# Attending and feeding forward the last 512 queries as two halves of 256, in a transformer block on one Trainium2 core

## Chip, cores, metric

One core of one Trainium2 chip runs the whole program. The metric is device time in microseconds of one launch; medians of several runs are quoted. The first profile of the kernel before was taken at a granted TensorE clock of 0.749 and spans 1417.9 us, where the timed runs take 1201 us.

In the profiles PE is TensorE (PEld its weight loads), ACT is ScalarE, DVE is VectorE and POOL is GpSimd. PSUM is the memory that this kernel's matmuls write, in eight banks.

## The reference

A pre-layernorm transformer block: 2048 tokens, width 1024, 32 heads of 32, feed-forward width 3584, bfloat16.

```python
x = A_x                                         # 1 x 2048 x 1024
h = x + attention(layernorm(x)) @ wo            # qkv = layernorm(x) @ wqkv, 32 heads, full softmax
out = h + gelu(layernorm(h) @ w1 + b1) @ w2 + b2
```

## The kernel before

The program builds a graph of tasks (groups of instructions with what they read and write), plans it with a list scheduler that has a price for each task, and emits each engine's instructions in the order of that plan. The plan's times do not reach the chip; only the order does.

Queries go in four chunks of 512 (`qc`). For each chunk and pair of heads, PE computes scores in row tiles (contraction of 32), ACT takes exponentials of 128 x 1024 at a time (256 of them per chunk), and PE multiplies these with V and with ones, in column tiles ("PV"). The output projection (`wo`), layernorm and feed-forward of chunk `qc - 1` are background: they fill PE's time inside the attention of chunk `qc`. There they have one PSUM bank (bank 7; banks 0 to 5 hold scores, 6 the sums of PV), and use four weight tiles of 32 columns side by side, so that they share a tiling mode with PV. The last chunk has no attention after it; its `wo`, layernorm and feed-forward are the tail, with eight banks and the full 128 x 128 array.

```python
# (cut) a background matmul: narrow while attention runs, full in the tail
if narrow:   # four 32-column tiles, side by side: "a group"
    for j in range(4): p.matmul(psum[32*j:32*j+32, bank, c0:c1], lhsT[:, 32*j:32*j+32], rhs, tile_position=(0, 32*j), ...)
    pe(fns, occ, ..., mode="col")
else:
    pe(lambda p: p.matmul(psum[:, bank, c0:c1], lhsT, rhs, ...), occ, ..., mode="full")

# (cut) the order of the program
for qc in range(1, NCH):
    ...
    wo(R1, qc - 1, [7], R1); ln2(R1, qc - 1, [7], ...); ffn1(R1, qc - 1, [7]); ffn2(R1, qc - 1, [7])
    attention_chunk(qc)
    attention_flush()
al = [0, 1, 2, 3, 4, 5, 6, 7]
wo(R1, NCH - 1, al, R2); ln2(R2, NCH - 1, al); ffn1(R2, NCH - 1, al); ffn2(R2, NCH - 1, al)

# (cut) who gets PE next, in the plan
if "qk" in best: return best["qk"]                                   # scores first
...
if "pv" in best and (... waiting >= PV_FORCE ...): return best["pv"]
if "bg" in best: return best["bg"]                                   # what is left: background
```

In the plan a change of PE's tiling mode (row tiles, column tiles, full array) costs 0.1 us (`switch=0.1`) and a group of 512 columns 0.2195 us.

The softmax here doesn't subtract the row's maximum and nothing guards it: scores larger than these inputs give would overflow.

Of the kernel before, what the change touches and what calls it, by code (L numbers as in the profile page):

```python
# [284 lines left out]
def build_kernel(nc, A_x, A_wqkv, A_wo, B_w1, B_b1, B_w2, B_b2, out):  # L285
# [72 lines left out]
    PT, B_PT = sb(top, "PT", [P, NPT, 2, 512], BF, NPT)  # L358
    ot_lo = Area(top.cur)
# [19 lines left out]
    gT, B_gT = sb(ffn, "gT", [P, FC, 512], BF, FC)  # L379

    class Rings:


        def __init__(self, area, pfx, nw1, nw2, ngl, nos, nx, nxb):
# [3 lines left out]
            self.w1, self.B_w1 = sb(area, pfx + "w1r", [P, nw1, DC, 256], BF, nw1)  # L388
            w2_area = Area(area.cur + 3 * 4096)
            self.w2, self.B_w2 = sb(area, pfx + "w2r", [P, nw2, 4, 512], BF, nw2)  # L390

            if nw2 == 7:
                self.xq, self.B_xq = sb(w2_area, pfx + "xq", [P, DC, 512], BF)
                self.hnT, self.B_hnT = sb(w2_area, pfx + "hnT", [P, DC, 512], BF, 1, 4)
            self.xb, self.B_xb = sb(area, pfx + "xb3", [P, self.nxb, D], BF, self.nxb)
# [171 lines left out]
    def load_q(qc, g):  # L567
        n = qc * G + g
        s = n % NQ
        if n < 2:  # L570
            return
        for half in range(2):
            dma(QT2[64 * half:64 * half + 64, s, :, :], qd[g, qc].rearrange("(pr r) t -> r pr t", pr=2), 64 * 2048,
                reads=[B_qd[g][qc]], writes=[B_QTh[s][half][0], B_QTh[s][half][1]], prio=-1)

    def late_q(R, qc, gs):

        dma(R.xq[:, :, :], xd[qc - 1], P * 8192, reads=[B_xd[qc - 1]], writes=[R.B_xq], prio=0)
        for g2 in range(gs // 2, G // 2):
            s = wblock(R, A_wqkv[:, 256 * g2:256 * g2 + 256], 0)  # L580
            for k in range(2):
                g = 2 * g2 + k
                for dc in range(DC):
                    mm(7, R.w1[:, s, dc, k * P:k * P + P], R.xq[:, dc, :], dc == 0, dc == DC - 1,
                       [R.B_w1[s], R.B_xq], True)
                o = R.next("os", R.nos)
                dve(lambda v, o=o: v.tensor_copy(R.ost[:, o, :], psum[:, 7, :]), c_dve_ps(512),
                    reads=[B_ps[7]], writes=[R.B_ost[o]])
                dma(qd[g, qc], R.ost[:, o, :], P * 1024, reads=[R.B_ost[o]], writes=[B_qd[g][qc]], prio=0)
# [19 lines left out]
    class Att:  # L609


        def __init__(self):
# [4 lines left out]
            self.fin = set()  # L617

        def qk(self, qc, units):

            fns, banks, rd, us = [], [], [], []
            for p16, kt in units:
                tc, k4 = divmod(kt, 4)
                half, i = divmod(k4, 2)
                g, pr = divmod(p16, 2)
                qs = (qc * G + g) % NQ
                u = self.unit % self.n_units
                self.unit += 1
                us.append(u)
                for j in range(2):  # L630
                    r0 = 64 * half + 32 * j

                    def fn(p, j=j, r0=r0, u=u, p16=p16, tc=tc, i=i, qs=qs, pr=pr):
                        return p.matmul(psum[:, 2 * u + j, :], KT2[r0:r0 + 32, p16, tc, i, :],  # L634
                                        QT2[r0:r0 + 32, qs, pr, :], start=True, stop=True, tile_position=(r0, 0))
                    fns.append(fn)
                banks += [B_ps[2 * u], B_ps[2 * u + 1]]
                rd += [B_KT[4 * p16 + tc][half], B_QTh[qs][half][pr]]
            pe(fns, 0.224, reads=rd, writes=banks, kind="qk", mode="row")
            for (p16, kt), u in zip(units, us):  # L640
# [4 lines left out]
                self.pv.append((qc, p16, kt, s))  # L645

        def pv_unit(self, bank, first, last):
            qc, p16, kt, s = self.pv[self.done]
            self.done += 1
            g, pr = divmod(p16, 2)  # L650
            fns = []
            for j in range(2):
                h = 2 * p16 + j
                fns.append(lambda p, j=j, h=h: p.matmul(  # L654
                    psum[32 * j:32 * j + 32, bank, :], V[:, kt, 32 * h:32 * h + 32], PT[:, s, j, :],
                    start=first, stop=last, tile_position=(0, 32 * j), skip_group_check=True))
            for j in range(2):
                fns.append(lambda p, j=j: p.matmul(  # L658
                    psum[64 + 32 * j:96 + 32 * j, bank, :], ones32[:, :], PT[:, s, j, :],
                    start=first, stop=last, tile_position=(0, 64 + 32 * j), skip_group_check=True))  # L660
            pe(fns, 0.224, reads=[B_PT[s], B_V[4 * kt + (p16 // 4)], B_ones], writes=[B_ps[bank]], kind="pv", mode="col")
            if last:
                self.finish(qc, g, pr, bank)

        def finish(self, qc, g, pr, bank):
            dve(lambda v: v.tensor_copy(Dsb[64 * pr:64 * pr + 64, :], psum[64:128, bank, :]), c_dve_ps(512),  # L666
                reads=[B_ps[bank]], writes=B_Dsb[pr], prio=-1)
            dve(lambda v: v.tensor_copy(Osb[64 * pr:64 * pr + 64, :], psum[0:64, bank, :]), c_dve_ps(512),  # L668
                reads=[B_ps[bank]], writes=[B_Osb[pr]], prio=-1)
            self.fin.add((qc, g, pr))  # L670
            if (qc, g, 1 - pr) in self.fin:
                for k in range(4):
                    dve(lambda v, k=k: v.reciprocal(Dsb[:, 128 * k:128 * k + 128], Dsb[:, 128 * k:128 * k + 128]), 0.93,  # L673
                        reads=[B_Dsb[0][k], B_Dsb[1][k]], writes=[B_Dsb[0][k], B_Dsb[1][k]], prio=1)
                    if qc == NCH - 1 and g == G - 1:
                        c = slice(128 * k, 128 * k + 128)
                        dve(lambda v, c=c: v.tensor_tensor(OT[:, qc % 2, g, c], Osb[:, c], Dsb[:, c], ALU.mult), c_dve(128),
                            reads=[B_Dsb[0][k], B_Dsb[1][k]] + B_Osb, writes=[B_OT[qc % 2][g][k]], prio=1)
                if not (qc == NCH - 1 and g == G - 1):
                    dve(lambda v: v.tensor_tensor(OT[:, qc % 2, g, :], Osb[:, :], Dsb[:, :], ALU.mult), c_dve(512),  # L680
                        reads=B_Dsb[0] + B_Dsb[1] + B_Osb, writes=B_OT[qc % 2][g], prio=1)
# [5 lines left out]
    def attention_round(qc, p16, r):  # L687
        tc, i = divmod(r, 2)
        att.qk(qc, [(p16, 4 * tc + i), (p16, 4 * tc + 2 + i)])
        while len(att.pv) - att.done > PV_LAG:  # L690
            att.pv_unit(6, att.done % 16 == 0, att.done % 16 == 15)

    def attention_flush():
        while len(att.pv) > att.done:
            att.pv_unit(6, att.done % 16 == 0, att.done % 16 == 15)


    def wblock(R, src_ap, prio=1):
        s = R.next("w1", R.nw1)
        dma(R.w1[:, s, :, :], src_ap.rearrange("(dc p) c -> p dc c", p=P), P * DC * 512, writes=[R.B_w1[s]], prio=prio)  # L700
        return s

    def wo(R, qc, banks, RX):
        nb = 0
        R.cnt["w1"] += -R.cnt["w1"] % 4
        ws = [wblock(R, A_wo[:, 256 * k:256 * k + 256]) for k in range(4)]
        assert ws == [0, 1, 2, 3]
        for t4 in range(4):
            for j in range(2):
# [3 lines left out]
                tt = qc * 4 + t4  # L713
                for k, g in enumerate([7, 0, 1, 2, 3, 4, 5, 6] if len(banks) == 1 else range(G)):
                    mm(bank, OT[:, qc % 2, g, t4 * P:(t4 + 1) * P], R.w1[:, s:s + 2, g, :], k == 0, k == 7,
                       [B_OT[qc % 2][g][t4], R.B_w1[s], R.B_w1[s + 1]], len(banks) == 1)
# [6 lines left out]
    def ln2(R, qc, banks, between=None):  # L723
        nb = 0
        for t4 in range(4):
# [9 lines left out]
    def ffn1(R, qc, banks):  # L735
        nb = 0
        for blk in range(FC // 2):
            s = wblock(R, B_w1[:, 256 * blk:256 * blk + 256])
            for f in range(2):
                fc = 2 * blk + f  # L740
                bank = banks[nb % len(banks)]
                nb += 1
                for dc in range(DC):
                    mm(bank, R.w1[:, s, dc, f * P:(f + 1) * P], R.hnT[:, dc, :], dc == 0, dc == DC - 1,
                       [R.B_w1[s]] + R.B_hnT, len(banks) == 1)
                i = R.next("gl", R.ngl)
                if len(banks) == 1:
                    dve(lambda v, i=i, fc=fc, bank=bank: v.tensor_scalar(R.xh[:, i, :], psum[:, bank, :], b1f[:, fc:fc + 1], None, ALU.add),  # L748
                        c_dve_ps(512), reads=[B_ps[bank], B_b1f], writes=[R.B_xh[i]])
                else:  # L750
                    act(lambda a, i=i, fc=fc, bank=bank: a.activation(R.xh[:, i, :], psum[:, bank, :], ACT.Identity,
                                                                      bias=b1f[:, fc:fc + 1], scale=1.0),
                        512, reads=[B_ps[bank], B_b1f], writes=[R.B_xh[i]], ap_bias=True)
# [6 lines left out]
                dve(lambda v, i=i, fc=fc: v.scalar_tensor_tensor(gT[:, fc, :], R.th[:, i, :], 1.0, R.xh[:, i, :], ALU.add, ALU.mult),  # L760
                    c_dve(512), reads=[R.B_th[i], R.B_xh[i]], writes=[B_gT[fc]], prio=1)

    def ffn2(R, qc, banks):
        nb = 0
        for j in range(2):
            ws = []
            for q in range(FC // 4):
                s = R.next("w2", R.nw2)
                dma(R.w2[:, s, :, :], B_w2[512 * q:512 * q + 512, 512 * j:512 * j + 512].rearrange("(f p) c -> p f c", p=P),
                    P * 4096, writes=[R.B_w2[s]], prio=1)  # L770
                ws.append(s)
            for t4 in range(4):
                bank = banks[nb % len(banks)]
                nb += 1
                tt = qc * 4 + t4
                mm(bank, two_row[:, :], b2t[:, 512 * j:512 * j + 512], True, False, [B_two, B_b2t], len(banks) == 1)
                for fc in range(FC):
                    s = ws[fc // 4]
                    mm(bank, gT[:, fc, t4 * P:(t4 + 1) * P], R.w2[:, s, fc % 4, :], False, fc == FC - 1,
                       [B_gT[fc], R.B_w2[s]], len(banks) == 1)  # L780
# [27 lines left out]
    seen = [0, 0]  # L808

    def lead_pv(n):  # L810
        while len(att.pv) - att.done > n:
            p16 = att.pv[att.done][1]
            seen[p16] += 1
            att.pv_unit(6 if p16 == 0 else 5, seen[p16] == 1, seen[p16] == NT)

    att.n_units = 2
    for tc in range(4):
# [14 lines left out]
        for k in range(4):  # L832
            att.qk(0, [(k % 2, 4 * tc + k // 2), (1 - k % 2, 4 * tc + 2 + k // 2)])
# [41 lines left out]
    def attention_chunk(qc, first=0):  # L875
        for p16 in range(first, 16):
            g, pr = divmod(p16, 2)
            if pr == 0:
                load_q(qc, g)
            for r in range(8):  # L880
# [126 lines left out]
```

## Time and profile before

| | kernel before |
|---|---|
| first three runs | 1201.17 us median (1200.93 to 1204.41) |
| first profile, at clock 0.749 | span 1417.9 us |
| second profile of the same kernel, at clock 0.990 | span 1202.6 us |
| its last exponential ends at | 1073.9 us |
| its tail, from there to the end | 128.7 us |

These lines are from the first profile's page: each engine's busy time, share of the span and instructions, then the granted clock in 40 equal slices, in tenths.

```profile
PE 1366.2 (96%) x17326; PEld 510.9 (36%) x17336; DVE 673.2 (47%) x1165; ACT 1085.3 (77%) x1189; POOL 37.9 (3%) x96
...
PEclk7777777777777777777777777777777777766777
```

PE is busy throughout and ACT three quarters: at that clock PE is the bound. The stretches view of the same profile, in the middle of an attention chunk, has 656 matmuls in 50 us. Its columns are: stretch, length, then busy time and instructions of PE, PEld, DVE, ACT and POOL, granted clock, DMA share, GB/s.

```profile
550.00:600.00 50.00, 49.36 (x656) 16.39 (x652) 13.00 (x18) 41.99 (x44) 0.00 (x0) 0.75 0.28 86
```

656 / 4 = 164 groups of 512 columns, at 0.284 us each by the granted clock, are 46.6 us, 93% of the 50: the "93% efficiency, about 20 ns lost per group" of the prediction.

The second profile (the kernel unchanged, submitted as the first experiment) is what the timed runs look like. The page's busy times, the last 512 queries' attention and the tail in the stretches view, then what waited longest in that attention:

```profile
PE 1129.5 (94%) x17336; PEld 465.6 (39%) x17336; DVE 668.5 (56%) x1165; ACT 1059.8 (88%) x1189; POOL 38.3 (3%) x96
```

```profile
816.00:1074.00 258.00, 241.11 (x3710) 88.72 (x3702) 142.22 (x225) 255.01 (x286) 6.23 (x16) 0.99 0.33 97
1074.00:1202.60 128.60, 117.26 (x551) 53.47 (x550) 71.08 (x130) 37.92 (x60) 6.46 (x16) 0.95 0.28 86
```

One period of that attention, from the timeline of PE (start, length, instruction, count; overlapping matmuls are pipelined, so only starts are exact):

```profile
999.53 1.04 PE L439 MATMUL ps<-a_w2r,gT 128*32 128x512 bf16 x16
1000.50 0.40 PE L634 MATMUL ps<-QT,KT 32*128 32x512 bf16 x4
1000.82 0.40 PE L439 MATMUL ps<-a_w2r,gT 128*32 128x512 bf16 x4
1001.05 0.38 PE L654 MATMUL ps<-PT,V 128*32 128x512 bf16 x2
...
1001.26 0.38 PE L654 MATMUL ps<-PT,V 128*32 128x512 bf16 x2
...
1001.48 0.82 PE L439 MATMUL ps<-a_w2r,gT 128*32 128x512 bf16 x12
1002.23 0.40 PE L634 MATMUL ps<-QT,KT 32*128 32x512 bf16 x4
```

Between two score groups (1000.50 to 1002.23, 1.73 us) PE runs seven groups: the scores, two of PV, four of the background. Groups of one mode start 0.216 us apart; the step into the scores and the step out of them take about 0.32 us. 7 x 0.216 + 2 x 0.11 = 1.73. The two exponentials of the period take ACT 2 x 0.924 = 1.85 us (48 back to back in 44.80 us less the last one's latency). So about 0.12 us of PE is free per period of 128: an estimate of some 15 us for the whole chunk from this one period. Periods differ: the next one, with eight groups, takes PE 1.96 us, more than the two exponentials.

### The profile page before, as it was taken

The numbers are of one execution on the slowest core, as the hardware profiler recorded it, in microseconds if no ns is written. First come the engines' busy times: TensorE is split into PE (matmuls) and PEld (weight loads), VectorE is DVE, ScalarE is ACT, GpSimd is POOL, SyncE is SP. The second block draws the span as 40 slices with busy tenths as digits, with TensorE's granted clock in tenths as the row PEclk, the third lists the DMA queues.
The fourth block names the chain that finished last, engine by engine and source line by source line (L and its number), as shares of the span: only waits on it lengthen the run. The fifth ranks groups of instructions, "written<-read, shape, count | busy, mean of one in ns | idle before, by whom it ended". The sixth has DMA issues, their size and how long they took to land.

```text
span 1417.9 us, 37847 instructions
## 1 busy us (share of the span) xinstructions
PE 1366.2 (96%) x17326; PEld 510.9 (36%) x17336; DVE 673.2 (47%) x1165; ACT 1085.3 (77%) x1189; POOL 37.9 (3%) x96
## 2 busy tenths in 40 slices
PE   8999999999999999999999999999999999978999
PEld 5544443433333333332333333333333333324333
DVE  7354444443546774223547762225677612245710
ACT  4778787878888888888888888888988888844500
POOL 2000000000100000000100000000000000001000
PEclk7777777777777777777777777777777777766777
DMA  6800000025343222303342230422323322202222
GB/s 165 224 2 13 28 13 14 13 72 156 101 122 101 76 69 72 124 16 98 107 124 71 83 98 16 124 71 63 107 73 98 102 66 85 87 0 75 74 93 71
DMA packets 165793, 112.29 MB, mean 79 GB/s; under 512 B 25345, under 2 KB 162817, under 8 KB 164866
## 3 DMA queue, kind: packets, MB, share of 16 engines
q1 hardware_dynamic: 165634, 109.87, 26.2%
q8 instruction: 136, 2.23, 0.7%
q14 instruction: 23, 0.19, 0.1%
HBM read 98.58 MB, written 11.27 MB: 77 GB/s over the span
## 4 chain that ended last, share of the span: by engine, by line
PE 91%; ACT 4%; DVE 3%; issue 1%; POOL 1%; DMA 0%; POOLq 0%; DVEq 0%
PE ps L439 48%; PE ps L654 17%; PE ps L634 12%; PE ps L443 10%; ACT PT L643 3%; PE ps L658 2%; PE ps L798 1%; ACT xnT L512 1%; DVE a_xh L748 1%; PE ps L508 1%; DVE V L606 0%; DVE stg L547 0%; DVE Osb L668 0%; DVE Dsb L666 0%; DMA a_w1r<-in_A_wqkv_dram 0%
## 5 line engine op out<-in xcount | busy, mean ns | idle before, releaser
L643 ACT ACTIVATE PT<-ps 128x1024 bf16<-128x1024 f32 x1024 | 989.2, 1025 | 180.5 <-PE ps L634 166.1
L654 PE MATMUL ps<-PT,V 128*32 128x512 bf16 x2048 | 383.4, 457 | 13.7 <-DVE V L606 6.2
L658 PE MATMUL ps<-PT,ones 128*32 128x512 bf16 x2048 | 384.8, 458 | 0.0
L439 PE MATMUL ps<-a_w2r,gT 128*32 128x512 bf16 x2688 | 241.9, 452 | 0.0
L634 PE MATMUL ps<-QT,KT 32*128 32x512 bf16 x2048 | 216.7, 414 | 7.4 <-ACT PT L643 7.3
L439 PE MATMUL ps<-a_hnT,a_w1r 128*32 128x512 bf16 x2688 | 215.2, 454 | 4.0 <-DVE a_xh L748 3.2
L654 PEld LDWEIGHTS ps<-PT,V 128*32 128x32 bf16 x2048 | 103.3, 104 | 143.9 <-issue 89.3
L634 PEld LDWEIGHTS ps<-QT,KT 32*128 32x128 bf16 x2048 | 51.5, 91 | 272.3 <-ACT PT L643 164.5
L439 PE MATMUL ps<-xnT,Wall 128*32 128x512 bf16 x1344 | 111.6, 453 | 7.0 <-ACT xnT L512 4.8
L439 PEld LDWEIGHTS ps<-a_w2r,gT 128*32 128x32 bf16 x2688 | 77.3, 109 | 112.0 <-issue 103.3
L673 DVE RECIPROCAL Dsb<-Dsb 128x128 f32<-128x128 f32 x128 | 115.1, 928 | 1.0
L439 PEld LDWEIGHTS ps<-a_hnT,a_w1r 128*32 128x32 bf16 x2688 | 70.6, 107 | 108.0 <-issue 71.4
L782 DVE SCALAR_TENSOR_TENSOR a_ost<-ps,hch 128x512 bf16<-128x512 f32 x24 | 16.6, 692 | 189.8 <-PE ps L439 189.7
L658 PEld LDWEIGHTS ps<-PT,ones 128*32 128x32 bf16 x2048 | 103.5, 104 | 6.6 <-issue 6.6
L748 DVE TENSOR_SCALAR a_xh<-ps,b1f 128x512 bf16<-128x512 f32 x84 | 63.1, 751 | 81.3 <-PE ps L439 80.2
L666 DVE COPY Dsb<-ps 64x512 f32<-64x512 f32 x64 | 44.4, 694 | 101.5 <-PE ps L658 100.1
L439 PE MATMUL ps<-Wall,xnT 128*32 128x256 bf16 x2048 | 83.8, 314 | 0.0
L547 DVE CAST stg<-ps 128x512 bf16<-128x512 f32 x40 | 27.5, 689 | 89.2 <-PE ps L439 89.2
L443 PE MATMUL ps<-a_hnT,b_w1r 128*128 128x512 bf16 x219 | 64.5, 470 | 2.1 <-ACT a_hnT L512 1.5
L439 PEld LDWEIGHTS ps<-Wall,xnT 128*32 128x32 bf16 x2048 | 57.6, 107 | 22.7 <-issue 11.3
L443 PE MATMUL ps<-a_w2r,gT 128*128 128x512 bf16 x219 | 64.1, 461 | 0.5
L439 PE MATMUL ps<-a_w1r,OT 128*32 128x512 bf16 x768 | 63.1, 453 | 0.8 <-DVE hch L719 0.5
(69 smaller groups left out, 875.5 us busy)
## 6 DMA issues: line engine op xcount, KB each, us to landing
a_w2r<-in_B_w_dram SPq DMA_DIRECT2D x56, 512.0 KB, 4.6
a_w1r<-in_B_w_dram SPq DMA_DIRECT2D x42, 512.0 KB, 3.9
a_w1r<-in_A_wo_dram SPq DMA_DIRECT2D x16, 512.0 KB, 4.7
QT<-q_scratch SPq DMA_DIRECT2D x60, 128.0 KB, 2.8
b_w1r<-in_B_w_dram SPq DMA_DIRECT2D x14, 512.0 KB, 3.8
a_w1r<-in_A_wqkv_dram SPq DMA_DIRECT2D x11, 512.0 KB, 5.1
xrb<-in_A_x_dram SPq DMA_DIRECT2D x16, 256.0 KB, 3.9
Wall<-in_A_wqkv_dram SPq DMA_DIRECT2D x16, 256.0 KB, 5.4
```

The lines of the kernel that those rows point to most:

```text
L439: fns.append(lambda p, j=j: p.matmul(psum[32 * j:32 * j + 32, bank, c0:c1], lhsT[:, 32 * j:32 * j + 32], rhs, start=start, stop=stop, tile ...
L443: pe(lambda p: p.matmul(psum[:, bank, c0:c1], lhsT, rhs, start=start, stop=stop), occ, reads=reads, writes=[B_ps[bank]], mode="full")
L508: pe(lambda p, dc=dc: p.transpose(psb[:, bank, dc * P:(dc + 1) * P], src_ap[:, dc * P:(dc + 1) * P], ident[:]), 0.064, reads=[B_src, B_ide ...
L547: dve(lambda v: v.tensor_copy(stg[:, s, :], psum[:, bank, :]), c_dve_ps(512), reads=[B_ps[bank]], writes=[B_stg[s]])
L634: return p.matmul(psum[:, 2 * u + j, :], KT2[r0:r0 + 32, p16, tc, i, :], QT2[r0:r0 + 32, qs, pr, :], start=True, stop=True, tile_position= ...
L643: act(lambda a, u=u, s=s: a.activation(PT[:, s, :, :], psum[:, 2 * u:2 * u + 2, :], ACT.Exp, bias=0.0, scale=SCALE), 1024, reads=[B_ps[2 * ...
L654: fns.append(lambda p, j=j, h=h: p.matmul(psum[32 * j:32 * j + 32, bank, :], V[:, kt, 32 * h:32 * h + 32], PT[:, s, j, :], start=first, st ...
L658: fns.append(lambda p, j=j: p.matmul(psum[64 + 32 * j:96 + 32 * j, bank, :], ones32[:, :], PT[:, s, j, :], start=first, stop=last, tile_po ...
L666: dve(lambda v: v.tensor_copy(Dsb[64 * pr:64 * pr + 64, :], psum[64:128, bank, :]), c_dve_ps(512), reads=[B_ps[bank]], writes=B_Dsb[pr], p ...
L673: dve(lambda v, k=k: v.reciprocal(Dsb[:, 128 * k:128 * k + 128], Dsb[:, 128 * k:128 * k + 128]), 0.93, reads=[B_Dsb[0][k], B_Dsb[1][k]], w ...
L748: dve(lambda v, i=i, fc=fc, bank=bank: v.tensor_scalar(R.xh[:, i, :], psum[:, bank, :], b1f[:, fc:fc + 1], None, ALU.add), c_dve_ps(512), ...
L782: dve(lambda v, o=o, t4=t4, j=j, bank=bank: v.scalar_tensor_tensor(R.ost[:, o, :], psum[:, bank, :], 0.5, hch[:, t4, 512 * j:512 * j + 512 ...
```

## The change

The intent: the tail is PE alone and ACT idle, the attention is ACT-bound; so attend the last 512 queries in two halves of 256, and feed the first half forward while the second is attended. Then only 256 queries are left for the tail. Scores and PV of a half run with 256 columns and two key tiles per exponential, so an exponential still has 128 x 1024 elements. `wo`, `w1` and `w2` are loaded once more. The rings of weight buffers in the tail grow. Core of the diff (the rest passes a chunk object in place of `qc`):

```diff
+    chunks = [Chunk(0, 0, 0, 4), Chunk(1, 1, 0, 4), Chunk(2, 2, 0, 4), Chunk(3, 3, 0, 2), Chunk(4, 3, 2, 2)]
...
-            pe(fns, 0.224, reads=rd, writes=banks, kind="qk", mode="row")
+            pe(fns, 0.224 if per == 1 else 0.25, reads=rd, writes=banks, kind="qk", mode="row")
...
-    def ffn1(R, qc, banks):
+    def ffn1(R, ch, banks):
+        N = ch.n
+        per = 512 // N
...
+                elif len(banks) == 1:
+                    dve(lambda v, ...: v.tensor_tensor(R.xh[...], psum[:, bank, :]..., b1f[:, fc:fc + 2]...broadcast, ALU.add), ...)
...
-    for qc in range(1, NCH):
-        if qc == 1:
+    for i in range(1, len(chunks)):
+        ch = chunks[i - 1]
+        if i == 1:
             late_q(R1, 1, 2)
-        wo(R1, qc - 1, [7], R1)
-        ...
-        attention_chunk(qc)
+        wo(R1, ch, [7], R1)
+        ln2(R1, ch, [7], (lambda i=i: late_q(R1, i + 1, 0)) if i + 1 < NCH else None)
+        ffn1(R1, ch, [7])
+        ffn2(R1, ch, [7])
+        attention_chunk(chunks[i])
         attention_flush()
...
-    R2 = Rings(att_area, "b_", 4, 1, 4, 4, 8, 4)
-    wo(R1, NCH - 1, al, R2)
-    ...
+    R2 = Rings(att_area, "b_", 6, 6, 4, 4, 4, 2, hn=2)
+    last = chunks[-1]
+    wo(R2, last, al, R2)
+    ln2(R2, last, al)
+    ffn1(R2, last, al)
+    ffn2(R2, last, al)
```

## The prediction

> **What bounds the kernel.** The timed runs (1201 us) and the profiled one (1417.9 us) are in different regimes. The core view grants the profiled run a mean clock of 0.749, and the tail's matmuls (49 in 14.08 us, chain view) are 287 ns apart. The Trainium skill, "TensorE: Matmul & The Clock Gate", section "Wait - 56ns, not 53.3ns?", gives 215.7 ns for such a matmul at the full clock; 287 x 0.75 = 215 agrees. Counting the matmul groups of the by-form list (four tiles side by side count once) I get about 957 us of streaming at full clock, 1278 us at 0.749. That exceeds 1201, so the timed runs must have a clock of about 0.9 to 1. In the profile PE is the bound everywhere (96% busy, ACT 77%). In the timed runs I expect ACT to bound the attention: 1024 exponentials at about 0.925 us back to back (18 in 16.6 us, timeline) = 947 us, plus 84 tanh at about 0.5 us and the lead-in is about 1030 us to the last exponential; then a tail of PE alone (wo, layernorm, both feed-forward matmuls of 512 queries), 163 us in the profile, about 137 us at full clock (520 matmuls x 0.216 = 112, plus about 25 of normalization and layernorm latency). 1030 + 137 = 1167 against 1201 leaves some 34 us of ACT stalls.
>
> **What the change does.** Half of the tail's queries move into attention. Tail: 512 to 256 queries: wo 7, ffn1 and ffn2 25 each, latencies about 18: about 76 us, so 61 us removed. Into the last 512 queries' attention go 260 matmul groups. PE there, at full clock: attention 82 us plus feed-forward of 512 queries 111 us is 193 us of streaming; windows in the profile stream at 93% efficiency, about 20 ns lost per group, so about 213 us. The moved half adds about 62, and halves of 256 columns (twice the instructions for scores and PV) about 5: 280 us. ACT there is 251 us, after the change 258 (14 more tanh). So the last attention window turns from ACT-bound (about 259 with stalls) to PE-bound (about 285): 26 us given back. Added weight traffic is one more pass over wo, w1, w2, 16.8 MB; about 120 GB/s in attention, and about 210 GB/s in the short tail, which the enlarged rings prefetch only in part: the early profile slices reached 224 GB/s, so that is tight but possible, perhaps 3 us.
>
> **Sum.** 61 - 26 - 3 is 32 us at full clock, about 1169 us. If the timed clock is nearer 0.9, attention is already PE-bound, moving PE work gains only idle gaps (ACT-only stretches of 14 us at the window ends, layernorm latency), and it is nearer 10 to 15 us. I say 1170 us, 1143 to 1196; faster by over 2% 0.58, within 2% 0.38, slower 0.04.
>
> **What would show it.** Tail after the last exponential: 163 to about 90 us in the profile (clock 0.75). The last 512 queries' attention, about 304 us in the profile, grows by 40 to 60 us, with PE at 95% and the exponentials spread thinner; the ACT-only stretch before the tail vanishes. Profiled span about 1390. PE busy total almost unchanged. In the tail few PE waits on weight DMAs.
>
> **What would make it wrong.** Halves of 256 columns costing more per column (weight loads no longer hidden) and a PE-bound window giving back all 61 us; the tail starved for weights at about 300 GB/s; the feed-forward's single bank and its DVE evacuation limiting how fast the extra work goes in; or PE having more room at full clock than I think, then 1145.

## More of the kernel before

```profile
PEld ps L634 <- ACT PT L643: 48.0, 100, 1.1
```

ACT is busy 255 of 258 us in the attention, so ACT bounds it, and PE 241 of 258: nearly as full. The last line says that PE's weight loads for scores waited for exponentials 100 times, 48 us in all, in pieces of half a microsecond. That is not idle time of PE: its matmuls were busy for 241 of the 258 us, so most of these waits passed while earlier matmuls still ran.

## The result

The changed kernel takes 1213.19 us (1211.72 to 1215.85, four runs) against 1202.35 us for the kernel before in the same rounds: ratio 1.0086, 95% interval 1.0068 to 1.0105. It is slower, by about 1%. (Ratios here are the mean of one kernel's fast runs over the mean of the other's in the same rounds, so not quite the ratio of the medians quoted.)

The profile after, in the lines that answer those of before: the page's busy times; the last 512 queries' attention, then what came after the last exponential in two parts; and the longest wait of PE in that attention.

```profile
PE 1134.0 (93%) x20209; PEld 513.4 (42%) x20212; DVE 686.6 (57%) x1219; ACT 1052.1 (87%) x1187; POOL 37.7 (3%) x96
```

```profile
816.00:1071.00 255.00, 244.31 (x5356) 116.95 (x5355) 158.41 (x281) 253.04 (x285) 8.10 (x23) 1.00 0.38 110
1071.00:1148.00 77.00, 60.35 (x1349) 36.35 (x1353) 42.93 (x75) 8.94 (x15) 2.60 (x6) 0.98 0.73 219
1148.00:1214.10 66.10, 57.24 (x416) 37.25 (x411) 30.10 (x53) 22.89 (x44) 1.52 (x4) 0.95 0.42 126
```

```profile
PEld ps L670 <- ACT PT L680: 33.5, 88, 0.7
```

The attention is as long as before (255 against 258 us). The tail of the second half is short, as meant (66 us). But between them lies a stretch of 77 us that the kernel before did not have: ACT has 15 instructions in it: the end of the last exponential and 14 tanh of a feed-forward. Its beginning in the timeline (the end of each line is the idle time before it and what ended it):

```profile
1075.52 3.32 PE L455 MATMUL ps<-a_hnT,a_w1r 128*32 128x256 bf16 x64 [0.99 <-DVE a_hnT L530]
1078.90 0.69 DVE L804 TENSOR_TENSOR a_xh<-ps,b1f 128x512 bf16<-128x512 f32 x1 [3.24 <-PE ps L455]
...
1079.65 1.93 PE L455 MATMUL ps<-a_hnT,a_w1r 128*32 128x256 bf16 x64 [0.80 <-DVE a_xh L804]
...
1081.63 0.69 DVE L804 TENSOR_TENSOR a_xh<-ps,b1f 128x512 bf16<-128x512 f32 x1 [0.85 <-PE ps L455]
...
1082.38 1.93 PE L455 MATMUL ps<-a_hnT,a_w1r 128*32 128x256 bf16 x64 [0.80 <-DVE a_xh L804]
```

This is the first half's first feed-forward matmul, in narrow tiles of 256 columns, its very first block. It starts after the last exponential, not inside the second half's attention. And it has one bank: 1.93 us of matmuls, then 0.80 us of waiting for DVE to empty the bank, 2.73 us per block of 256 features, 14 blocks. Then its second matmul follows until 1151 us, on the same bank. From 1071 to 1120 us PE waits 11.0 us for DVE to empty that bank (total, times, longest):

```profile
PE ps L455 <- DVE a_xh L804: 11.0, 13, 0.9
```

The windows and tails of all kernels run, from the list of exponentials in each trace (the window is from the start of the 769th to the end of the last):

| kernel | window, us | tail after it, us | median, us | ratio to before |
|---|---|---|---|---|
| before (e0_before) | 256.7 | 128.7 | 1204.06 | 1.0015 |
| changed | 254.7 | 143.0 | 1213.19 | 1.0086 |
| e1_ffn_wide | 254.5 | 125.7 | 1196.68 | 0.9954 |
| e2_halves_only | 254.3 | 127.8 | 1198.99 | 0.9971 |
| e3_no_ffn_c2 (wrong result) | 251.5 | 70.5 | 1139.16 | 0.9473 |
| e4_plan_after | 268.1 | 131.6 | 1240.75 | 1.0325 |
| e4_plan_before | 267.5 | 129.4 | 1237.96 | 1.0295 |
| e5_ffn_joint | 254.6 | 112.1 | 1184.86 | 0.9859 |
| e6_ffn_joint_plan | 266.6 | 111.0 | 1218.82 | 1.0137 |
| e7_dose_half | 271.6 | 127.4 | 1217.77 | 1.0113 |
| e7_dose_full | 292.6 | 128.3 | 1236.95 | 1.0271 |
| e8_plan_last | 267.1 | 133.4 | 1216.57 | 1.0103 |
| e10_force7 | 290.4 | 98.5 | 1207.64 | 1.0039 |
| e10_force8 | 322.0 | 71.3 | 1212.52 | 1.0073 |

Theory F: PE was already full beside the exponentials, so the first half's feed-forward had nowhere to go; since scores go first in the plan, it was pushed behind the attention, and there it runs in the form made for the inside, narrow and on one bank. Rivals: the 256-column halves are slow in themselves (H); or the first half's feed-forward is ready too late to enter, whatever the room (O).

### The profile page after: what moved, and what is told of

Read it like the earlier page. It is cut to its first block, busy times and chain, and to the rows that moved or that the text cites. A ratio compares the mean times of both kernels' runs of the same rounds, so it can differ in the third digit from the quotient of the medians.

```text
span 1214.1 us, 43745 instructions
## 1 busy us (share of the span) xinstructions
PE 1134.0 (93%) x20209; PEld 513.4 (42%) x20212; DVE 686.6 (57%) x1219; ACT 1052.1 (87%) x1187; POOL 37.7 (3%) x96
## 4 chain that ended last, share of the span: by engine, by line
PE 73%; ACT 12%; DVE 10%; DMA 3%; issue 1%; POOL 0%; SPq 0%; POOLq 0%; DVEq 0%
PE ps L455 44%; PE ps L696 13%; PE ps L670 11%; ACT PT L680 11%; PE ps L459 5%; DVE a_xh L801 3%; DMA a_w2r<-in_B_w_dram 1%; ACT xnT L528 1%; PE ps L863 1%; DVE a_uu L816 1%; DVE a_xh L804 1%; DMA q_scratch<-stg 1%; DVE gT L823 1%; DVE a_ost L847 1%; DVE Dsb L719 1%
## 5 line engine op out<-in xcount | busy, mean ns | idle before, releaser
L680 ACT ACTIVATE PT<-ps 128x1024 bf16<-128x1024 f32 x1024 | 966.7, 1037 | 33.0 <-PE ps L670 19.6
L696 PE MATMUL ps<-PT,V 128*32 128x512 bf16 (+1 forms) x2560 | 320.7, 339 | 12.2 <-DVE V L637 5.3
L700 PE MATMUL ps<-PT,ones 128*32 128x512 bf16 (+1 forms) x2560 | 320.7, 339 | 0.0
L455 PE MATMUL ps<-a_hnT,a_w1r 128*32 128x512 bf16 (+1 forms) x3584 | 203.1, 356 | 23.6 <-DVE a_xh L804 11.0
L670 PE MATMUL ps<-QT,KT 32*128 32x512 bf16 (+1 forms) x2560 | 203.0, 340 | 12.1 <-ACT PT L680 8.6
L455 PE MATMUL ps<-xnT,Wall 128*32 128x512 bf16 x1344 | 92.6, 386 | 8.7 <-ACT xnT L528 5.4
L818 ACT ACTIVATE a_th<-a_uu 128x512 f32<-128x512 bf16 x98 | 62.2, 636 | 41.3 <-DVE a_uu L816 40.6
L711 DVE COPY Dsb<-ps 64x512 f32<-64x512 f32 (+1 forms) x80 | 47.0, 587 | 86.7 <-PE ps L700 84.6
L823 DVE SCALAR_TENSOR_TENSOR gT<-a_th,a_xh 128x512 bf16<-128x512 f32 x98 | 66.1, 675 | 3.5 <-ACT a_th L818 3.1
L816 DVE SCALAR_TENSOR_TENSOR a_uu<-a_sq,a_xh 128x512 bf16<-128x512 bf16 x98 | 66.8, 683 | 1.9
```

The source lines that it names most:

```text
L455: fns.append(lambda p, j=j: p.matmul(psum[32 * j:32 * j + 32, bank, c0:c1], lhsT[:, 32 * j:32 * j + 32], rhs, start=start, stop=stop, tile ...
L670: return p.matmul(psum[:, 2 * u + j, N * i2:N * i2 + N], KT2[r0:r0 + 32, p16, tc, i, :], QT2[r0:r0 + 32, qs, pr, 0:N], start=True, stop=Tr ...
L680: act(lambda a, u=u, s=s: a.activation(PT[:, s, :, :], psum[:, 2 * u:2 * u + 2, :], ACT.Exp, bias=0.0, scale=SCALE), 1024, reads=[B_ps[2 * ...
L696: fns.append(lambda p, j=j, h=h, kt=kt, i2=i2, st=st, sp=sp: p.matmul(psum[32 * j:32 * j + 32, bank, 0:N], V[:, kt, 32 * h:32 * h + 32], P ...
L700: fns.append(lambda p, j=j, i2=i2, st=st, sp=sp: p.matmul(psum[64 + 32 * j:96 + 32 * j, bank, 0:N], ones32[:, :], PT[:, s, j, N * i2:N * i ...
L711: dve(lambda v: v.tensor_copy(Dsb[64 * pr:64 * pr + 64, 0:N], psum[64:128, bank, 0:N]), c_dve_ps(N), reads=[B_ps[bank]], writes=B_Dsb[pr][ ...
```

## The experiments

### e0_before: the kernel before again

No edit.

> The kernel before, unchanged, to get its profile at the full clock (the first one fell at a granted clock of 0.749). Theory F (PE was already full): time equal to before within 0.3%; the last exponential ends near 1065 us, the tail after it takes about 137 us, feed-forward matmuls run until within 25 us of the last exponential, and PE waits for exponentials (weight loads of the scores released by ACT) sum to no more than about 15% of the last 250 us of attention. Rival H (halves of 256 columns are themselves slow): the last exponential ends clearly earlier than the 1071 us of the changed kernel, by 8 us or more. My prediction on record had 38 us of idle PE in that window; then feed-forward matmuls would end 30 us or more before the last exponential.

Measured: ratio 1.0015 (1.0000 to 1.0030), and a profile at clock 0.990. The last exponential ends at 1073.9 us, later than the changed kernel's 1071.1: rival H is out by this alone. F's own numbers were partly missed: the end was put near 1065 us and the tail at 137 (128.7 measured). Its feed-forward matmuls end about 21 us before the last exponential, within the 25 us that F gave and not the 30 or more of the prediction. Waits of scores for exponentials are 48 us of 258, 19%, a little more than the 15% I gave F. They are waits of weight loads, most of them hidden: by the starts of its matmuls (the sum is below, under "Size") PE itself is idle for 28 us of this window, about 8 of them in front of scores. The prediction had 38.

### e1_ffn_wide: the spilled feed-forward, done wide

```diff
-        ffn1(R1, ch, [7])
-        ffn2(R1, ch, [7])
+        if i < 4:
+            ffn1(R1, ch, [7])
+            ffn2(R1, ch, [7])
         attention_chunk(chunks[i])
...
+    ffn1(RA, chunks[3], al)      # RA: the tail's rings, with the first half's layernorm output
+    ffn2(RA, chunks[3], al)
     wo(R2, last, al, R2)
```

> The changed kernel, but both feed-forward matmuls of the first half are put after the attention in program order, with all eight banks and full 128-column weights, instead of one bank and four narrow weight tiles. Theory F: the exponentials end at the same 1071 us (nothing that ran inside attention is taken out), the first half's feed-forward after them takes about 50 us instead of 75, and the time falls by 15 to 22 us against the changed kernel, to about 1195 us, ratio to before 0.990 to 0.998. If the first half's feed-forward had in part run inside the attention, taking it out costs time: ratio to before above 1.01.

Measured: 1196.68 us, ratio to before 0.9954. The window does not change (254.5 us), so nothing of this feed-forward had been inside it; the part after it shrinks by 17.3 us (143.0 to 125.7). So doing it wide wins back all of the loss of the change, and a little more. The edit changes several things together: eight banks, whole weight tiles, more weight buffers, and ACT instead of DVE to empty the banks. The 11.0 us of waits for the one bank are the largest part that the trace of the changed kernel names; the rest was not separated. In e1 the same matmuls run on without a wait for a bank:

```profile
1072.82 8.71 PE L459 MATMUL ps<-a_hnT,a_w1r 128*128 128x256 bf16 x64 [1.07 <-DVE a_hnT L530]
1081.37 2.89 PE L459 MATMUL ps<-a_hnT,b_w1r 128*128 128x256 bf16 x25
```

### e2_halves_only: the halves alone

```diff
-        wo(R1, ch, [7], R1)
-        ... ffn2(R1, ch, [7])
+        if i < 4:
+            wo(R1, ch, [7], R1)
+            ... ffn2(R1, ch, [7])
         attention_chunk(chunks[i])
...
-    wo(R2, last, al, R2)
+    last = Chunk(5, 3, 0, 4)     # all 512 queries, with the rings of the kernel before
+    wo(R1, last, al, R2)
```

> Only the attention of the last 512 queries in two halves of 256; output projection, layernorm and feed-forward of the 512 as before, in the tail. Theory F: the halves themselves cost little, time within 0.5% of before (1200 to 1208 us), exponentials end within 5 us of those of before. Rival H: the halves cost, time 1210 us or more, about all of the change's loss, exponentials later by 8 us or more.

Measured: 1198.99 us, ratio 0.9971 (0.9954 to 0.9988). The halves cost nothing; H falls. The small gain, 2 us of it in the window, I did not trace further.

### e3_no_ffn_c2: make room

```diff
-        ffn1(R1, ch, [7])
-        ffn2(R1, ch, [7])
+        if i == 3:               # wrong on purpose: rows 1024 to 1535 get the sum before the feed-forward
+            for t4 in range(4):
+                dma(out2[(8 + t4) * P:(9 + t4) * P, :], hch[:, t4, :], P * 2048, reads=[B_hch[t4]], prio=0)
+        else:
+            ffn1(R1, ch, [7])
+            ffn2(R1, ch, [7])
```

> Wrong result on purpose: the changed kernel with the feed-forward of the third 512 queries left out (its output is the sum before it), which empties 456 matmul groups out of the last 512 queries' attention. Theory F: now the first half's feed-forward does run inside the second half's attention; the exponentials end at 1050 to 1065 us, the tail after them is 65 to 75 us, time 1120 to 1140 us. Rival O (the first half's feed-forward cannot enter anyway, for its dependences come too late): the exponentials end there too, but the tail stays 120 to 143 us, time 1175 to 1205 us.

Measured: 1139.16 us; the exponentials end at 1068.2 us (F had 1050 to 1065) and the tail is 70.5 us. With the third chunk's feed-forward gone, the first half's went where it was meant to go: its first block leaves PSUM at 965 us and its last output at 1062 us, both before the last exponential:

```profile
965.41 0.69 DVE L804 TENSOR_TENSOR a_xh<-ps,b1f 128x512 bf16<-128x512 f32 x1 [2.83 <-PE ps L455]
...
1062.05 0.69 DVE L847 SCALAR_TENSOR_TENSOR a_ost<-ps,hch 128x512 bf16<-128x512 f32 x1 [1.29 <-PE ps L455]
```

Dependences allow it, so O falls; it was room that lacked. (The comparison with the reference still calls this kernel correct: it does not see a missing feed-forward of 512 queries, so "correct" is a weak statement for this part of the program.)

### e4_plan_after and e4_plan_before: a plan that packs more

The prediction's idle time could have been there and merely left unused by a cautious plan. One constant makes the plan think that mode switches are cheap, so that it puts more background between two scores:

```diff
-    gr.schedule(pick_pe)
+    gr.schedule(pick_pe, switch=0.03)
```

> The changed kernel with one constant of its own planner altered: the price of switching PE between row tiles, column tiles and the full array from 0.10 to 0.03 us. The engines' order is fixed by that plan, so it now puts more feed-forward groups between two score groups. Theory F1 (PE is really full beside the exponentials): the exponentials are pushed apart, end later by about what is gained behind them, and the time stays within 0.7% of the changed kernel's 1213 us (1205 to 1220). Theory F2 (there was room, some 36 us of waits for exponentials in the last 260 us of attention, but the plan's price of a switch left it unused): less feed-forward is left after the last exponential, and the time falls by 10 to 30 us, to 1183 to 1203 us.

> The kernel before with the same altered constant. F1: within 0.7% of before. F2: little to gain here, for its feed-forward ends within the attention anyway, only the earlier stages can run closer: 1190 to 1202 us; the feed-forward of the third 512 queries then ends 30 us or more before the last exponential.

Measured: 1240.75 us and 1237.96 us, 2.3% and 2.9% above the same kernels with the plan's own constant. Both theories' numbers were missed, F2's in direction: the exponentials end 36 us and 32 us later, and far less is gained behind them. The constant acts on all stages: the 769th exponential, where the last chunk begins, already starts 22 us later than in the kernels with the plan's own constant (838.7 against 816.4 us in the changed one), so most of the loss was made in earlier stages. But the last window is longer too, and in e4_plan_before no work had been added to it: 267.5 us against 256.7 in e0_before. Its feed-forward ends 42 us before the last exponential, as F2 had it, and the exponentials still end later. So this order of the same work costs some 11 us in one window by itself. Remember this for e8, which repeats the edit for the last chunk alone.

The granted clock is not the reason. In e4_plan_before it falls to 0.50 for 17 to 20 us near each change of chunk, where background has run out, but ACT is full there (558.5 to 578.7 us: busy 19.6 of 20.2 us). Where the background runs, from 845 to 1064 us, the clock is 1.00 and ACT is idle for 9.4 of 219.0 us; in e0_before, from 817.2 to 1053 us, for 2.8 of 235.8.

### e5_ffn_joint and e6_ffn_joint_plan: a version meant to beat both

e5 keeps what fits inside (the first half's `wo` and layernorm) and puts all feed-forward behind the attention, wide. The first matmul goes in halves from one load of the weights, so that the first half's part fills PE while the second half's layernorm is computed; the second matmul does all 512 at once.

```diff
-    R2 = Rings(att_area, "b_", 6, 6, 4, 4, 4, 2, hn=2)
+    R2 = Rings(att_area, "b_", 14, 0, 4, 2, 2, 2, hn=-1)     # all 14 blocks of w1 stay
...
-    ffn1(R2, last, al)
-    ffn2(R2, last, al)
+    ws = [wblock(R2, B_w1[:, 256 * blk:256 * blk + 256]) for blk in range(FC // 2)]
+    ffn1(R2, chunks[3], al, ws)
+    ffn1(R2, last, al, ws)
+    ffn2(R2, Chunk(5, 3, 0, 4), al)
```

> A version meant to beat both: two halves of attention as in the change, the first half's output projection and layernorm inside the second half's attention, but both feed-forward matmuls after the attention with all banks; the first one in halves of 256 columns from one load of the weights (the first half's fills the wait for the second half's layernorm), the second one for all 512. Exponentials end at 1068 to 1071 us as in e1; tail 448+8+32 matmul-equivalents of 0.216 us, 105 us, plus about 8: time 1180 to 1188 us, ratio to before 0.981 to 0.988. If layernorm waits were not on the tail's chain, it is no better than e2 (1199 us).

> e5 with the planner's price of a switch at 0.03 us. F2: 8 to 20 us under e5. F1: within 0.7% of e5.

Measured: e5 1184.86 us, ratio 0.9859 (0.9842 to 0.9875), the best version: 1.4% under before, 2.3% under the changed kernel. (e3 is shorter, but leaves work out.) Its tail is 112.1 us. Compare the start of the tail of before, where PE waits 5.84 us for a layernorm, with that of e5, where the first half's matmuls run on through it:

```profile
1076.05 11.18 PE L443 MATMUL ps<-a_w1r,OT 128*128 128x512 bf16 x51
1093.07 1.89 PE L508 MATMUL ps<-ident,b_xb 128*128 128x128 bf16 x16 [5.84 <-DVE b_xb L502]
```

```profile
1075.21 3.83 PE L460 MATMUL ps<-a_w1r,OT 128*128 128x512 bf16 x17
1078.88 3.98 PE L460 MATMUL ps<-a_hnT,b_w1r 128*128 128x256 bf16 x35
1082.70 0.61 PE L525 MATMUL ps<-ident,b_xb 128*128 128x128 bf16 x8
1083.14 4.20 PE L460 MATMUL ps<-a_hnT,b_w1r 128*128 128x256 bf16 x37
```

The waits are not all of the gain. The tail before was granted a clock of 0.95 on average, 0.50 from 1092.5 to 1102.6 us, that of e5 1.00 (1071 to 1183 us); how much of the 16.6 us by which the tail is shorter is due to each was not separated.

e6 is 1218.82 us: the cheap-switch plan costs 34 us here too.

### e7_dose_half and e7_dose_full: how much PE work fits beside the exponentials

The kernel before, with matmuls of zero weights added to the sums of PV in the last chunk, after every second PV unit or after each. The plan does not know of them.

```diff
+            if qc == 3 and not last and self.done % 2 == 0:      # full: % 1
+                for j in range(4):
+                    fns.append(lambda p, j=j: p.matmul(
+                        psum[32 * j:32 * j + 32, bank, :], zero32[:, :], PT[:, s, 0, :],
+                        start=False, stop=False, tile_position=(0, 32 * j), skip_group_check=True))
```

> The kernel before, with extra PE work that changes no result put into the last 512 queries' attention: 112 groups of four narrow matmuls with zero weights, one after every second PV unit, adding zero to the same accumulation; the plan does not know of them, so the order is unchanged. They are 112 x 0.216 = 24 us of PE. My prediction on record said that PE has some 38 us idle in this window: then the exponentials' end moves by under 5 us and the time by under 0.5%. If the idle pieces ahead of the scores (45 us summed in the profile of before) can't be used, the window stretches by nearly the whole dose: 17 to 26 us, time 1219 to 1229 us.

> The same after every PV unit: 240 groups, 52 us, about as much PE work as the 260 groups that the change meant to move. With 38 us of room: 10 to 18 us longer (1213 to 1222 us). With none: 42 to 55 us longer (1244 to 1258 us).

Measured: the window grows by 14.9 us for 24 us of dose, and by 35.9 us for 52 us (256.7 to 271.6 and 292.6). Both fall between the two sets of numbers I had written. So the room for extra work, in this place and form, is 9 to 16 us, not 38 and not nothing. That agrees with the 15 us of the period above. An added group costs 0.13 to 0.15 us, not its full 0.216.

### e8_plan_last: the packing plan in the last chunk only

```diff
-                            start += switch
+                            start += switch if now < 817.0 else 0.03
```

> The changed kernel with the planner's price of a switch lowered to 0.03 us only from the last 512 queries' attention on, so all earlier stages keep their order: part of the first half's feed-forward then really goes between the scores of the second half. If a group costs more inside the saturated attention than behind it (about 0.29 us a group read from the earlier altered plan, against 0.216 on the full array behind it and about 0.3 on one bank behind it), the exponentials end 6 to 12 us later, the tail is shorter by about as much, and the time is within 0.7% of the changed kernel (1205 to 1221 us). If there is room, it is 1185 to 1203 us.

Measured: 1216.57 us. The exponentials end at 1081.0 us, 9.9 us later than in the changed kernel; the part behind them is 9.6 us shorter. Within the window there are now 198 narrow matmuls of 256 columns of the first half's feed-forward, about 50 groups, where there were none: the window is 12.4 us longer, 0.25 us for each of these groups of 256 columns, and what is behind the attention is shorter by 0.19 us for each. The plan does not pay. But the 0.25 us is no price of a moved group: e4_plan_before's window grew by 10.8 us under the same constant with nothing moved into it.

### e10_force8 and e10_force7: do what the change was meant to do

Open after this was whether only the placement had failed (then forcing the work inside should pay what was predicted) or also the cost of a moved group.

```diff
+        if "qk" in best and num[best["qk"]] >= num[qks[384]] and "bg" in best and state.get("bg", 0.0) < 8.0:   # or 7.0
+            state["bg"] = state.get("bg", 0.0) + best["bg"].occ / MM
+            return best["bg"]
         if "qk" in best:
+            state["bg"] = 0.0
             return best["qk"]
```

> The changed kernel, but from the last 512 queries' attention on the plan puts background groups (as many as are ready, up to 8 of 512 columns) between one pair of score groups and the next before it takes the next scores; by the plan none of the first half's feed-forward is then left after the last exponential. This does what the change was meant to do. What my prediction on record had: window 285 us, tail 76 us, time 1169 us. What the doses say (240 more groups cost 34 us) with the moved half's 14 tanh: exponentials end 35 to 50 us later than the changed kernel's 1070 us, at 1105 to 1120 us, tail after them 64 to 72 us, time 1170 to 1192 us, ratio to before 0.973 to 0.991. If a group really costs 0.24 to 0.29 us inside as in the altered plans (260 groups: 62 to 75 us), the exponentials end at 1132 to 1145 us and the time is 1197 to 1215 us: then nothing is to be had from doing it inside, wherever it is placed.

> The same with up to 7 groups: by the plan 140 of the background's matmul groups on one bank are left behind the last exponential instead of 340. Between the changed kernel and the forced 8: by the doses 1185 to 1203 us; by 0.24 to 0.29 us a group 1203 to 1216 us.

Measured: with 8 the whole of the first half's feed-forward is inside, and the tail is 71.3 us, as the prediction had it (76). But the window is 322 us. The stretches of this kernel, attention and tail, and the two waits that face each other in the attention:

```profile
817.00:1139.80 322.80, 303.15 (x6717) 151.19 (x6710) 194.19 (x343) 268.36 (x299) 9.21 (x24) 0.99 0.49 143
1139.80:1211.10 71.30, 62.09 (x396) 39.06 (x394) 36.07 (x66) 22.91 (x44) 3.11 (x8) 0.92 0.35 100
```

```profile
ACT PT L680 <- PE ps L670: 48.3, 73, 2.2
...
PEld ps L670 <- ACT PT L680: 41.3, 86, 1.2
```

Now ACT waits 48 us for scores, and the weight loads of scores still wait 41 us for exponentials. The 228 moved groups (112 of the first matmul, counted in 512 columns, and 116 of the second) make the window 67.3 us longer: 0.295 us each, the waits of this order included. Removing them from behind saves 71.7 us. The time is 1212.52 us, that of the changed kernel. With 7 it is 1207.64 us, a little better, still above before. Both are in the range written for the expensive group.

## Why the prediction was wrong

It said 1170 us (1143 to 1196), 58% for faster by over 2%. Measured were 1213 us, 1% slower. Point by point:

- **Which regime the timed runs are in: right.** From 957 us of streaming it was inferred that the timed runs cannot have the profiled clock of 0.749 and that ACT bounds the attention in them. The second profile has clock 0.990 and ACT busy 255 of 258 us.
- **The tail: right.** 137 us were estimated for before and 76 after; 128.7 were measured, and 66 (second half's part of the changed kernel) to 71 (e3, e10_force8).
- **Halves of 256 columns cost little: right** (e2).
- **Starving for weights: not the cause.** The traffic behind the attention is about what was feared (219 GB/s in the 77 us stretch), but e1 moves the same bytes after the last exponential and is 17 us shorter. e1 also has more weight buffers, so this alone is not proof; in the changed kernel's stretch the waits for weights are at most 4 us (0.9 of PE, 3.1 of its weight loads), against 11.0 for the bank.
- **The step that failed: "So the last attention window turns from ACT-bound (about 259 with stalls) to PE-bound (about 285): 26 us given back."** It is wrong in two ways, and each alone takes the gain away.
  - *Placement.* It took for granted that moved work runs inside, and that the attention stretches to hold it. The plan does the contrary: scores first, background in what is left. Of the moved work only the 32 groups of `wo` and part of the layernorm went in. The window stayed at 255 us; the 228 feed-forward groups ran behind it in the inside's narrow form on one bank, for 77 us, and cost 17 us more than wide (e1). 63 us removed from the tail (128.7 to 66), 77 added in front of it: 143.0 against 128.7 us after the last exponential, with 2 us won in the window.
  - *Size.* The window with the work really inside is 322 us, not 285: 67 us given back, not 26 (e10_force8). The prediction read the window off PE's load, as if PE would then never wait. PE's load can be summed from the shortest distances between matmul starts in the traces: 0.216 us for a group of 512 columns, 0.109 for one of 256, and 0.106 and 0.11 more for a mode switch into scores and out of them. The window before has 921 groups of 512 columns (199 us), 32 transposes of 128 columns (2 us) and 127 pairs of switches (27 us): some 229 us of 256.7, so about 28 us of idle time (a few us at half clock count as idle in this sum). The prediction had 213 us and 38: its "about 20 ns lost per group" had been read off a stretch at the low clock. In e10_force8 the same sum gives 285 us, and the prediction had 280. That this agrees is luck: the load before was 16 us too low, the added load 11 us too high (62 and 5 estimated, 56 found). What failed is the step from load to window: PE is still idle for about 37 of the 322 us, and ACT waits 48 us for scores at other times. Of the 28 us of idle time before, only 9 to 16 us took extra work (e7).
- **What would make it wrong** named "a PE-bound window giving back all 61 us" and the single bank. The first is what e10_force8 shows (67 us), the second what the changed kernel shows.

What stays open: e7's zero-weight groups cost 0.15 us apiece next to PV, the real ones 0.295 us for 512 columns (e10_force8). The difference is waiting, not matmul time: by the same sum PE's load in e7_dose_full's window is 281 us, nearly that of e10_force8, and PE is idle for 12 us of 292.6, not 37 of 322. Real groups need the bank emptied by DVE, weights from HBM and 14 more tanh on ACT, and were bunched up to eight at a time; which of these makes the waits was not separated. An order that interleaves them as finely as the doses might do better than e10; none was tried.

## What to carry to other kernels

Before moving work under another engine's shadow, count what PE does in one period of the steady state, mode switches included, and compare it with the other engine's period: here PE's own work already filled 1.73 us of ACT's 1.85 in a period. The sum of PE's loads is a lower bound for the new window, not a forecast of it: the waits between the engines come on top (37 us in e10_force8). And do not take a wait of a weight load for idle time of PE. In a kernel with a fixed order, also ask where the moved work goes if it does not fit; here it came out behind the attention in a form chosen for the inside, and cost more than at its old place. What did pay was to move only the latency-bound pieces (output projection, layernorm) and to let the first half's wide matmuls cover the second half's layernorm: 1.4%, with the halves (0.3%, e2) and the steadier clock of that tail included.

## What the Trainium skill lacked or had wrong

- "TensorEngine Tiling (Array Packing)", section "Key Properties", says that changing the tiling mode drains the array, but gives no cost. Here a switch into row tiles adds 0.106 us and one back to column tiles 0.11 us to the 0.216 us between groups of 512 columns: 27 us in one chunk of attention.
- "TensorE: Matmul & The Clock Gate", section "Wait — 56ns, not 53.3ns?", has 215.7 ns between matmuls of 512 columns at the full clock; this agrees (0.216 us); nothing is wrong here.
- The same page, Part 1, knows granted clocks of 4/8, 8/8 and, with three busy cores of a die, 13/16, and mentions one stuck at 1/4. The first profile of the kernel before was granted 0.75 for 1242 us without a break, with one core in use; no page has this state, nor does any run here show what sets it. It made that profile 18% longer than the timed runs and hid that ACT is the bound.
- The same page's summary asks for no gaps in PE's work over about 3 us to keep the clock, and this is not enough here. In e3_no_ffn_c2 matmuls never started more than 0.9 us apart between 845 and 945 us, and the clock was still at 0.5 for stretches of 13.7, 23.9 and 17.1 us. The page's section "A second HAM failure mode: psum-queue depth-cycling" reports the like for frequent short idle pieces; it gives no measure of how much idle is too much, and no run here tests it. The stretch, with the clock in the third column from the end:

```profile
900.00:925.00 25.00, 21.10 (x332) 6.84 (x336) 6.91 (x12) 25.00 (x29) 0.00 (x0) 0.57 0.05 13
```

- "Perfetto Trace Analysis", section "Matmul Optimizations", advises to use all eight PSUM banks, and gives no figure. One bank cost 11.0 us of waits in one feed-forward of 256 queries here; the 17 us of e1 have other changes in them as well.
